# Sinkhorn's column sum behind the second product of a block, its row scaling ahead of the last one, and the first expert's row weights earlier

## The chip, the cores and the metric

The kernel runs on one core of a Trainium2 chip. The metric is the device time of one execution in microseconds (us), and less is better. TensorE is called PE in the rows, VectorE DVE, ScalarE ACT, GpSimd POOL; PEld is TensorE's weight load.

## The reference, cut to what matters

Three stages follow each other: linear attention, a soft mixture of experts, and a second mixture of experts with a Sinkhorn gate. The change touches the last one alone:

```python
logits = x @ w_gate                       # x [2304, 512], w_gate [512, 8]
P = np.exp(logits - logits.max())
for _ in range(8):
    P /= P.sum(1, keepdims=True) + 1e-09  # rows: over the 8 experts
    P /= P.sum(0, keepdims=True) + 1e-09  # columns: over the 2304 tokens
    P *= N / E
for e in range(E):                        # 8 experts
    h = np.maximum(x @ w1[e], 0.0)
    out += P[:, e:e + 1] * (h @ w2[e])
```

## The kernel before

The second mixture runs as 8 experts times 9 blocks of 256 tokens, expert by expert; a block is two row groups of 128 tokens. The matrix product with w2 is done by a Winograd-like scheme in **seven products** (k = 0 to 6) of twelve matmuls each: 4 chunks, each as high part by high weight, high by low, low by high. `PRODUCTS` names for each k the operand (`a11`, `a12`, `s2`, `s1`, `s3`, `s4`, `a22`), the weight part and the running sum (`x`, `z`, `x`, `y`, `x`, `y`, `x`). After each product `take(i, k)` adds the running sum to a quarter of the output tile `xo`. So `x` is read by a take after products 0, 2, 4 and 6, and the next product on `x` cannot write before that read is done. In expert 0 the takes that are first in their quarter are copies on ScalarE (k = 0, 2, 3 and 6) and the others adds on VectorE (k = 1, 4, 5). In experts 1 to 7 all takes are on VectorE and multiply by the token's weight, `xo += P * sum`.

While block i's products run, block i+1's operands are made. After product 2 come the eight matmuls of `first_layer` (z1, then z0), and the generator `hidden` is advanced by one step after each of products 2 to 6: ScalarE makes `r` and the high parts `hh_a`, `hh_s`, VectorE the sums `s1`, `s2`, `s4`, `s3` and the low parts `hl_a`, GpSimd the low parts `hl_s`. The sums and `r` share three buffers.

The next expert's weights are prepared beside this: `W_PARTS` and `W_SUMS` give the (block, product) after which a weight part is cast on ScalarE and its low part made on GpSimd, or a sum of two weights made on GpSimd.

**Sinkhorn** has no stage of its own. It is the generator `sinkhorn`, of which `SINK` advances so many steps after a product, in expert 0 alone. One of the 8 iterations has five steps: (1) row sums `rs`, plus 1e-9, reciprocal; (2) `P` times `rs`; (3) column sums `cs` within each of the 128 partitions; (4) a product with a matrix of ones, `pcs`, that sums over partitions, plus 1e-9, reciprocal, times N / E; (5) `P` times `cs`. With `SINK = {0: 1, 1: 2, 6: 2}` steps 2 and 3 stand after product 6, step 4 after product 0 of the next block, and steps 5 and 1 after its product 1. `pcs` goes into the PSUM tile of z0. The last column sum is in block 8.

`P` is final only at the end of expert 0. Expert 0's `xo` is therefore summed without weight and multiplied by `P[:, t, 0]` afterwards, in `scale_rows`: row groups 0 and 1 after product 4 of expert 0's block 8, the two row groups of each later block behind the last product of the block ahead of it, in expert 1.

From the end of the attention on, every engine works in program order (`InOrder`), so the order in which this loop is written is the order on each engine, and an instruction that waits holds up all that is behind it on its engine.

Of the kernel before, what the change touches and what calls it, by code (L numbers as in the profile page):

```python
# [9 lines left out]
AF = mybir.ActivationFunctionType  # L10
ALU = mybir.AluOpType
# [5 lines left out]
NTOK, DM = B * S, H * D  # L17
NT = NTOK // 128
E, SPE, FF = 8, 4, 1024
# [34 lines left out]
def tile_kernel(ctx: ExitStack, tc: tile.TileContext, a):  # L54
    nc = tc.nc
    PE, V, A, G, SP = nc.tensor, nc.vector, nc.scalar, nc.gpsimd, nc.sync
# [386 lines left out]
    for i in range(NT + LAG + 1):  # L443
        t = i - LAG
# [60 lines left out]
    PE, V, A, G, SP = (InOrder(tc, x) for x in (PE, V, A, G, SP))  # L505
# [93 lines left out]
    NBLK = NT // 2  # L599
# [18 lines left out]
    def w_begin(e):  # L618
        u = [w2_unit("moe2_w2", e, n) for n in range(2)]
        t = cl1.tile([128, KH, 256], F32, tag="t", name=f"t{e}")  # L620
        b11, b12, b21 = u[0][:, :, 0:256], u[0][:, :, 256:512], u[1][:, :, 0:256]
        wsrc[e] = {"b11": b11, "b21": b21, "b22": u[1][:, :, 256:512], "t1": b11, "t2": t, "t3": b12, "t4": b21}
# [31 lines left out]
    def load_munits(n):  # L654
        for _ in range(n):
            if nm[0] < len(munits):
                load_unit(wa, *munits[nm[0]])
                nm[0] += 1
# [64 lines left out]
    xo = cp.tile([128, NT, DM], F32, name="xo")  # L723
    P = cp.tile([128, NT, E], F32, name="P")

    def acc_tile(name):
        return pm.tile([128, 512], F32, tag="m", name=name)

    def z_tile(n, name):
        return pz.tile([128, 1024], F32, tag=f"z{n}", name=name)  # L730
# [17 lines left out]
    def spread_stack(st, e):  # L748

        hl = st[:, FF // 2:].rearrange("p (n f) -> p n f", n=2)  # L750
        for n in range(2):
            pr = z_tile(n, f"pr{e}_{n}")
            for part in range(2):
                for j in range(2):
                    PE.matmul(pr[:, j * 256:(j + 1) * 256], rep[n][:, 2 * j + part, :], hl[:, part, :], start=part == 0 and j == 0, stop=part == 1, skip_group_check=True)
            A.copy(out=st[:, n * 512:(n + 1) * 512], in_=pr[:, 0:512])

    def sinkhorn():

        pg = acc_tile("pgate")  # L760
        for c in range(KC):
            PE.matmul(pg[:, 0:E], sot[:, c, :], wg[:, c, :], start=c == 0, stop=c == KC - 1)
        gst = cp.tile([128, E], F32R, name="gst")
        V.tensor_copy(out=gst, in_=pg[:, 0:E])
        V.tensor_tensor(out=gst[64:128, :], in0=pg[64:128, 0:E], in1=gst[64:128, :].bitcast(F32), op=ALU.subtract)
        yield
        pl = acc_tile("plog")
        for t in range(NT):
            PE.matmul(pl[:, t * E:(t + 1) * E], ct[t // 4][:, t % 4 * 128:(t % 4 + 1) * 128], gst, start=True, stop=True)
        yield  # L770
        Pf = P.rearrange("p t e -> p (t e)")
        V.tensor_copy(out=Pf, in_=pl[:, 0:NT * E])
        gm = cp.tile([128, 1], F32, name="gm")
        V.tensor_reduce(out=gm, in_=Pf, axis=AX.X, op=ALU.max)
        yield
        pg = acc_tile("pgm")
        PE.transpose(pg[0:1, 0:128], gm, ident)
        gm1 = cp.tile([1, 1], F32, name="gm1")
        V.tensor_reduce(out=gm1, in_=pg[0:1, 0:128], axis=AX.X, op=ALU.max)
        pg = acc_tile("pgb")  # L780
        PE.matmul(pg[:, 0:1], ones[0:1, :], gm1, start=True, stop=True)
        yield
        V.tensor_copy(out=gm, in_=pg[:, 0:1])
        V.tensor_scalar_sub(Pf, Pf, gm)
        A.activation(out=P, in_=P, func=AF.Exp)
        yield
        for it in range(8):
            rs = cp.tile([128, NT, 1], F32, tag="rs", name=f"rs{it}")
            V.tensor_reduce(out=rs, in_=P, axis=AX.X, op=ALU.add)
            V.tensor_scalar_add(rs, rs, 1e-9)  # L790
            V.reciprocal(out=rs, in_=rs)
            yield
            V.tensor_tensor(out=P, in0=P, in1=rs.to_broadcast([128, NT, E]), op=ALU.mult)
            yield
            cs = cp.tile([128, 1, E], F32, tag="cs", name=f"cs{it}")
            csf = cs.rearrange("p o e -> p (o e)")
            V.tensor_reduce(out=csf, in_=P.rearrange("p t e -> p e t"), axis=AX.X, op=ALU.add)
            yield
            pg = z_tile(0, f"pcs{it}")
            PE.matmul(pg[:, 0:E], ones, csf, start=True, stop=True)  # L800
            V.tensor_scalar_add(csf, pg[:, 0:E], 1e-9)
            V.reciprocal(out=csf, in_=csf)
            V.tensor_scalar_mul(csf, csf, float(NTOK) / E)
            yield
            V.tensor_tensor(out=P, in0=P, in1=cs.to_broadcast([128, NT, E]), op=ALU.mult)
            yield
# [74 lines left out]
    def product(i, k):  # L881
        e, blk = blocks[i]
        a, _, to = PRODUCTS[k]
        if (i, to) not in sums:
            sums[i, to] = acc_tile(f"{to}_{i}")[:, 0:256]
            fresh = True
        else:
            fresh = False
        h, l = hop.pop((i, a))
        w = wop[e, k]  # L890
        ps = sums[i, to]
        for c in range(KH):
            PE.matmul(ps, h[:, c], w[:, 0, c], start=fresh and c == 0, stop=False, skip_group_check=True)
            PE.matmul(ps, h[:, c], w[:, 1, c], start=False, stop=False, skip_group_check=True)
            PE.matmul(ps, l[:, c], w[:, 0, c], start=False, stop=c == KH - 1, skip_group_check=True)
        if blk == NBLK - 1:
            wop.pop((e, k))

    def take(i, k):

        e, blk = blocks[i]
        ps = sums[i, PRODUCTS[k][2]]
        r, c = TAKES[k]
        t = 2 * blk + r
        o = xo[:, t, c * 256:(c + 1) * 256]
        if e == 0:
            if (r, c) in [TAKES[j] for j in range(k)]:
                V.tensor_tensor(out=o, in0=ps, in1=o, op=ALU.add)
            else:
                (V.tensor_copy if blk == NBLK - 1 else A.copy)(out=o, in_=ps)  # L910
        else:
            V.scalar_tensor_tensor(out=o, in0=ps, scalar=P[:, t, e:e + 1], in1=o, op0=ALU.mult, op1=ALU.add)
        if e == E - 1 and k == 5:
            SP.dma_start(out=a["out"][t * 128:(t + 1) * 128, :], in_=xo[:, t, :])
        if e == E - 1 and (r, c) in ((1, 0), (1, 1)) and k in (4, 6):
            SP.dma_start(out=a["out"][t * 128:(t + 1) * 128, c * 256:(c + 1) * 256], in_=o)

    def scale_rows(blk):
        for t in (2 * blk, 2 * blk + 1):
            A.activation(out=xo[:, t, :], in_=xo[:, t, :], func=AF.Copy, scale=P[:, t, 0:1])  # L920

    sums = {}
    blocks = [(e, blk) for e in range(E) for blk in range(NBLK)]
# [14 lines left out]

    W_SUMS = {(3, 1): 0, (3, 6): 1, (5, 6): 2, (7, 6): 3}
    W_PARTS = {(2, 6): 0, (4, 6): 2, (6, 6): 1, (8, 1): 3, (8, 6): 4, (9, 0): 5, (9, 1): 6}  # L940
    SINK = {0: 1, 1: 2, 6: 2}
    making = iter(())
    for i, (e, blk) in enumerate(blocks):
        more = e + 1 < E
        if blk == 2 and more:
            w_begin(e + 1)
        for k in range(7):
            product(i, k)
            take(i, k)
            if k == 0 and blk == NBLK - 1 and more:  # L950
                stacks[e + 1] = make_stack(e + 1)
            if k == 1 and blk == NBLK - 1 and more:
                spread_stack(stacks[e + 1], e + 1)
            if k == 2 and i + 1 < len(blocks):
                first_layer(i + 1, 1)
                first_layer(i + 1, 0)
                making = hidden(i + 1)
            next(making, None)
            if more and (blk, k) in W_SUMS:
                w_sum(e + 1, W_SUMS[blk, k])  # L960
            if more and (blk, k) in W_PARTS:
                w_part(e + 1, W_PARTS[blk, k])
            if e and (blk + 9, k) in W_PARTS:
                w_part(e, W_PARTS[blk + 9, k])
            if e == 0:
                for _ in range(SINK.get(k, 0) - (blk == 0 and k == 1)):
                    next(sink, None)
            if k == 4 and i + 1 == NBLK:
                scale_rows(0)
        if i + 1 < len(blocks) and blocks[i + 1][0] == 1 and i + 1 > NBLK:  # L970
            scale_rows(blocks[i + 1][1])
        for to in "xyz":
            sums.pop((i, to))
        if blk == 0 and e and more:
            load_munits(4)
# [62 lines left out]
```

## Time and profile before

| | us |
|---|---|
| median of 3 runs | 1099.89 |
| lowest and highest | 1097.52, 1102.34 |
| the profiled execution, its own time | 1099.17 |
| its span, first to last instruction | 1097.0 |
| TensorE busy in the span | 1053.4 |
| expert 0 of the second mixture, its 9 blocks | about 281 to 398 |
| expert 1 | about 398 to 501 |

A matmul's busy time overlaps that of the next one, so TensorE's busy share says little; what counts is the time from the start of a product to the start of the next, and the waits before single instructions. A timeline row gives the start in us from the span's start, the duration, the engine, the line, the operation, output and inputs with shapes, and in brackets the idle time before it with what ended it. Line 50 is a helper that records every operation, so the rows are told apart by their tiles.

### The profile page before, as it was taken

The numbers are of one execution on the slowest core, as the hardware profiler recorded it, in microseconds if no ns is written. First come the engines' busy times: TensorE is split into PE (matmuls) and PEld (weight loads), VectorE is DVE, ScalarE is ACT, GpSimd is POOL, SyncE is SP. The second block draws the span as 40 slices with busy tenths as digits, with TensorE's granted clock in tenths as the row PEclk, the third lists the DMA queues.
The fourth block names the chain that finished last, engine by engine and source line by source line (L and its number), as shares of the span: only waits on it lengthen the run. The fifth ranks groups of instructions, "written<-read, shape, count | busy, mean of one in ns | idle before, by whom it ended". The sixth has DMA issues, their size and how long they took to land.

```text
span 1097.0 us, 23161 instructions
## 1 busy us (share of the span) xinstructions
PE 1053.4 (96%) x9206; PEld 982.4 (90%) x9206; DVE 737.7 (67%) x1526; ACT 569.1 (52%) x1009; POOL 686.8 (63%) x442
## 2 busy tenths in 40 slices
PE   7999999999888899999999999999999999999998
PEld 4788889853888889999999999999999999999998
DVE  6878677750678866766776677567666766676765
ACT  5665544313455556655455455545554564555542
POOL 4776551107555676767767686867677775777443
PEclk9999989999999999999999999999999999999999
DMA  7762215379400040012002200400220022000111
GB/s 261 261 257 85 59 30 208 139 303 370 154 1 1 2 143 12 2 50 105 1 1 78 78 2 1 149 6 2 77 78 1 1 82 73 1 1 21 45 53 59
DMA packets 22571, 89.26 MB, mean 81 GB/s; under 512 B 2752, under 2 KB 5568, under 8 KB 14272
## 3 DMA queue, kind: packets, MB, share of 16 engines
q1 hardware_dynamic: 22176, 87.26, 22.0%
q8 instruction: 73, 1.20, 0.5%
q0 software_dynamic: 288, 0.52, 0.2%
q14 instruction: 34, 0.28, 0.1%
HBM read 83.05 MB, written 4.72 MB: 80 GB/s over the span
## 4 chain that ended last, share of the span: by engine, by line
PE 68%; POOL 15%; issue 6%; DVE 6%; ACT 4%; DMA 1%; SPq 0%; POOLq 0%; ACTq 0%; DVEq 0%
PE x L50 25%; PE y L50 12%; PE z L50 11%; POOL hl_s L50 8%; PE num L271 6%; POOL w_t L50 4%; PE kvacc L179 3%; POOL w_b L50 2%; DVE s L50 2%; PE ut L246 1%; PE ps L50 1%; PE kvp L218 1%; DMA moe_w<-in_moe_w 1%; ACT hh_s L50 1%; DVE xo L50 1%
## 5 line engine op out<-in xcount | busy, mean ns | idle before, releaser
L50 POOL TENSOR_TENSOR hl_s<-s,hh_s 128x512 fp32r<-128x512 f32 x288 | 367.4, 1297 | 240.9 <-ACT hh_s L50 226.5
L50 PE MATMUL x<-w_t,hh_s 128*128 128x256 f32 x1152 | 205.0, 278 | 5.2 <-DVE xo L50 3.9
L50 ACT ACTIVATE hh_s<-s 128x512 fp32r<-128x512 f32 x288 | 175.3, 629 | 52.0 <-DVE s L50 49.3
L50 PEld LDWEIGHTS x<-w_t,hh_s 128*128 128x128 f32 x1152 | 173.9, 188 | 7.2 <-issue 3.2
L50 DVE SCALAR_TENSOR_TENSOR xo<-x,P,xo 128x256 f32<-128x256 f32 x252 | 121.0, 480 | 81.0 <-PE x L50 75.4
L50 ACT ACTIVATE hh_a<-z 128x512 fp32r<-128x512 f32 x216 | 122.2, 600 | 90.5 <-DVE s L50 88.6
L50 ACT ACTIVATE r<-z 128x512 f32<-128x512 f32 x144 | 86.2, 599 | 159.9 <-PE z L50 159.6
L50 DVE SCALAR_TENSOR_TENSOR s<-z,r 128x512 f32<-128x512 f32 x144 | 99.0, 688 | 90.6 <-ACT hh_a L50 86.2
L50 PE MATMUL x<-w_t,hl_s 128*128 128x256 f32 x576 | 159.7, 277 | 0.0
L50 DVE SCALAR_TENSOR_TENSOR hl_a<-z,hh_a 128x512 fp32r<-128x512 f32 x216 | 147.2, 681 | 0.0
L50 DVE SCALAR_TENSOR_TENSOR s<-z,s 128x512 f32<-128x512 f32 x144 | 98.4, 684 | 20.6 <-POOL hl_s L50 19.3
L50 PE MATMUL x<-w_t,hh_a 128*128 128x256 f32 x576 | 104.3, 279 | 5.2 <-POOL w_t L50 4.8
L50 PEld LDWEIGHTS x<-w_t,hl_s 128*128 128x128 f32 x576 | 108.2, 188 | 0.0
L50 PE MATMUL y<-w_b,hh_s 128*128 128x256 f32 x576 | 103.9, 279 | 0.0
L50 PE MATMUL z<-w_b,hh_a 128*128 128x256 f32 x576 | 103.6, 280 | 0.0
L50 PE MATMUL x<-w_b,hh_a 128*128 128x256 f32 x576 | 103.4, 280 | 0.0
L50 PE MATMUL y<-w_t,hh_s 128*128 128x256 f32 x576 | 102.9, 278 | 0.0
L50 PEld LDWEIGHTS x<-w_t,hh_a 128*128 128x128 f32 x576 | 87.6, 188 | 6.8 <-POOL w_t L50 6.2
L50 PEld LDWEIGHTS z<-w_b,hh_a 128*128 128x128 f32 x576 | 87.3, 189 | 2.5 <-issue 2.5
L50 PEld LDWEIGHTS y<-w_b,hh_s 128*128 128x128 f32 x576 | 87.5, 188 | 1.3 <-POOL w_b L50 1.3
L50 PEld LDWEIGHTS x<-w_b,hh_a 128*128 128x128 f32 x576 | 88.0, 190 | 0.0
L50 PEld LDWEIGHTS y<-w_t,hh_s 128*128 128x128 f32 x576 | 87.6, 189 | 0.0
(214 smaller groups left out, 2344.7 us busy)
## 6 DMA issues: line engine op xcount, KB each, us to landing
moe_w<-in_moe_w SPq DMA_DIRECT2D x64, 1024.0 KB, 6.9
vt<-in_vb SPq DMA_DIRECT2D x20, 256.0 KB, 3.6
kt<-in_kT SPq DMA_DIRECT2D x18, 256.0 KB, 3.5
qt<-in_qT SPq DMA_DIRECT2D x18, 256.0 KB, 2.7
out<-xo SPq DMA_DIRECT2D x18, 128.0 KB, 1.7
out<-xo SPq DMA_DIRECT2D x9, 256.0 KB, 2.0
rep<-in_rep POOLq DMA_DIRECT2D x2, 256.0 KB, 6.0
bd<-in_bd SPq DMA_DIRECT2D x1, 384.0 KB, 3.7
```

The costliest lines, as they stand in the source:

```text
L50: return lambda *args, **kwargs: self.tc.keep_in_program_order(make(*args, **kwargs))
L179: PE.matmul(acc[64 * j:64 * j + 64, p * 256:(p + 1) * 256], v[:, (2 * p + j) * D:(2 * p + j + 1) * D], phik[:, 2 * p + j].rearrange("p c f ...
L218: PE.matmul(ps[:, c * 192:(c + 1) * 192], kvt[:, p * 256 + c * 128:p * 256 + (c + 1) * 128], bd[:, p], start=True, stop=True)
L246: PE.transpose(ps[:, j * 128:(j + 1) * 128], uq_t[t][hh][:, j * 128:(j + 1) * 128], ident)
L271: PE.matmul(ps[r0:r1, j * XW:(j + 1) * XW], phiq[:, c, j * 128 + r0:j * 128 + r1], kvs_t[b][:, c, 4 * hh + j, :], start=c == 0, stop=c == 1,)
```

## The change

`SINK` becomes `{1: 3, 5: 2}`. Steps 2 and 3 stand after product 5 now, steps 4, 5 and 1 after product 1 of the next block (in block 0 the first two steps that stood after products 0 and 1 both stand after product 1). In step 4 the addition of 1e-9 and a multiplication by E / N are one instruction ahead of the reciprocal, and the multiplication behind it is gone: eight VectorE instructions fewer in all. `scale_rows` becomes `scale_row`: row group 0 is weighted after product 3 and row group 1 after product 4 of expert 0's block 8; the two row groups of block b+1 are weighted after products 0 and 1 of block b of expert 1, where they were weighted after its product 6.

```diff
             pg = z_tile(0, f"pcs{it}")
             PE.matmul(pg[:, 0:E], ones, csf, start=True, stop=True)
-            V.tensor_scalar_add(csf, pg[:, 0:E], 1e-9)
+            V.tensor_scalar(out=csf, in0=pg[:, 0:E], scalar1=1e-9, scalar2=float(E) / NTOK, op0=ALU.add, op1=ALU.mult)
             V.reciprocal(out=csf, in_=csf)
-            V.tensor_scalar_mul(csf, csf, float(NTOK) / E)
             yield
...
-    def scale_rows(blk):
-        for t in (2 * blk, 2 * blk + 1):
-            A.activation(out=xo[:, t, :], in_=xo[:, t, :], func=AF.Copy, scale=P[:, t, 0:1])
+    def scale_row(t):
+        A.activation(out=xo[:, t, :], in_=xo[:, t, :], func=AF.Copy, scale=P[:, t, 0:1])
...
-    SINK = {0: 1, 1: 2, 6: 2}
+    SINK = {1: 3, 5: 2}
...
-            if k == 4 and i + 1 == NBLK:
-                scale_rows(0)
-        if i + 1 < len(blocks) and blocks[i + 1][0] == 1 and i + 1 > NBLK:
-            scale_rows(blocks[i + 1][1])
+            if i == NBLK - 1 and k in (3, 4):
+                scale_row(k - 3)
+            if e == 1 and k in (0, 1) and blk + 1 < NBLK:
+                scale_row(2 * (blk + 1) + k)
```

In the orders that follow the number behind a name is a serial number of the tile. On **VectorE** in expert 0, around the end of block 1, where block 2's operands are made, the order before is this (`xo<-y` is take 5, `s_2_3593` is s3, `hl_a_2_3589` the low part of a22, `xo<-z` take 1 of block 2):

```order
L50 TENSOR_TENSOR xo<-y_3528,xo 128x256
L50 SCALAR_TENSOR_TENSOR s_2_3593<-z_0_2_3516,r_2_3565 128x512
L50 SCALAR_TENSOR_TENSOR hl_a_2_3589<-z_0_2_3511,hh_a_2_3587 128x512
L50 TENSOR_TENSOR P<-P,rs_3494 128x144
L50 TENSOR_REDUCE cs_3615<-P 128x8
L50 TENSOR_SCALAR cs_3615<-pcs_3632 128x8
L50 RECIPROCAL cs_3615<-cs_3615 128x8
L50 TENSOR_SCALAR cs_3615<-cs_3615 128x8
L50 TENSOR_TENSOR xo<-z_3637,xo 128x256
L50 TENSOR_TENSOR P<-P,cs_3615 128x144
```

and now:

```order
L50 TENSOR_TENSOR xo<-y_3527,xo 128x256
L50 SCALAR_TENSOR_TENSOR s_2_3592<-z_0_2_3515,r_2_3564 128x512
L50 TENSOR_TENSOR P<-P,rs_3493 128x144
L50 TENSOR_REDUCE cs_3596<-P 128x8
L50 SCALAR_TENSOR_TENSOR hl_a_2_3588<-z_0_2_3510,hh_a_2_3586 128x512
L50 TENSOR_TENSOR xo<-z_3631,xo 128x256
L50 TENSOR_SCALAR cs_3596<-pcs_3645 128x8
L50 RECIPROCAL cs_3596<-cs_3596 128x8
L50 TENSOR_TENSOR P<-P,cs_3596 128x144
```

Row scaling and column sums moved ahead of the low part of a22, the reading of `pcs` behind take 1, and the multiplication behind the reciprocal is gone.

On **TensorE** at the start of block 1 of expert 0 (`x<-w_b` is product 0, `z<-w_b` product 1, `x<-w_t,hh_s` product 2) the order before is

```order
L50 MATMUL x_3460<-w_b_2944,hh_a_1_3366 128x256 x2
L50 MATMUL x_3460<-w_b_2944,hl_a_1_3368 128x256
L50 MATMUL pcs_3474<-cs_3458,ones 128x8
L50 MATMUL z_3479<-w_b_3076,hh_a_1_3387 128x256 x2
L50 MATMUL z_3479<-w_b_3076,hl_a_1_3389 128x256
```

and now:

```order
L50 MATMUL z_3474<-w_b_3076,hh_a_1_3387 128x256 x2
L50 MATMUL z_3474<-w_b_3076,hl_a_1_3389 128x256
L50 MATMUL pcs_3488<-cs_3440,ones 128x8
L50 MATMUL x_3460<-w_t_3039,hh_s_1_3409 128x256 x2
L50 MATMUL x_3460<-w_t_3039,hl_s_1_3411 128x256
```

`pcs` moved from between products 0 and 1 to between products 1 and 2. On **ScalarE** from block 8 of expert 0 to block 0 of expert 1 (the names with 9 belong to the operands of expert 1's block 0, `CAST` are weight parts, `xo<-xo,P` is the weighting of a row group, `r_10` begins the operands of block 1) the order before is

```order
L50 ACTIVATE hh_s_9_4691<-s_9_4670 128x512
L50 ACTIVATE hh_s_9_4710<-s_9_4686 128x512
L50 ACTIVATE r_9_4709<-z_1_0_4660 128x512
L50 ACTIVATE xo<-xo,P 128x512 x2
L50 ACTIVATE hh_a_9_4733<-z_1_0_4655 128x512
L50 ACTIVATE hh_s_9_4736<-s_9_4716 128x512
L50 ACTIVATE hh_s_9_4755<-s_9_4739 128x512
L50 CAST w_t_4760<-moe_w_1_0_3298 128x1024
L50 CAST w_b_4777<-moe_w_1_1_3300 128x1024
L50 CAST w_t_4794<-moe_w_1_1_3300 128x1024
L50 ACTIVATE r_10_4820<-z_1_1_4810 128x512
```

and now:

```order
L50 ACTIVATE xo<-xo,P 128x512
L50 ACTIVATE hh_s_9_4703<-s_9_4678 128x512
L50 ACTIVATE r_9_4702<-z_1_0_4652 128x512
L50 ACTIVATE xo<-xo,P 128x512
L50 ACTIVATE hh_a_9_4725<-z_1_0_4647 128x512
L50 ACTIVATE hh_s_9_4728<-s_9_4709 128x512
L50 ACTIVATE hh_s_9_4747<-s_9_4731 128x512
L50 CAST w_t_4752<-moe_w_1_0_3298 128x1024
L50 CAST w_b_4769<-moe_w_1_1_3300 128x1024
L50 ACTIVATE xo<-xo,P 128x512
L50 CAST w_t_4787<-moe_w_1_1_3300 128x1024
L50 ACTIVATE xo<-xo,P 128x512
```

The first two weightings moved apart, and two more, of block 1's row groups, stand in block 0 of expert 1 already. In the later blocks of expert 1 two weightings stand where two stood, but for the row groups of the block that follows. On GpSimd and SyncE the order is the same.

## Rows read from the trace of the kernel before

**Rows 1.** Blocks: stretch, length, busy PE, PEld, DVE, ACT, POOL; clock, DMA.
```profile
307.11:319.48 12.37, 10.97 (x97) 10.80 (x96) 8.54 (x19) 6.09 (x14) 5.12 (x5) 1.00 0.00 1
319.48:332.60 13.12, 11.35 (x96) 10.98 (x95) 12.07 (x19) 7.27 (x15) 10.00 (x7) 1.00 0.00 1
...
420.97:431.45 10.48, 10.48 (x95) 10.48 (x93) 7.30 (x15) 6.27 (x13) 5.10 (x4) 1.00 0.00 0
431.45:442.57 11.12, 10.74 (x94) 10.55 (x93) 7.28 (x15) 7.20 (x13) 9.86 (x6) 1.00 0.01 1
```

**Rows 2.** TensorE's waits, 390 to 480 us: total us, times, longest us.
```profile
PE x L50 <- DVE xo L50: 1.8, 4, 0.7
```

**Rows 3.** Timeline of TensorE, from product 0 to the first layer of block 2, expert 0.
```profile
308.36 0.28 PE L50 MATMUL x<-w_b,hl_a 128*128 128x256 f32 x1
310.04 0.36 PE L50 MATMUL pcs<-cs,ones 128*128 128x8 f32 x2 [1.40 <-DVE cs L50]
310.25 0.49 PE L50 MATMUL z<-w_b,hh_a 128*128 128x256 f32 x2
...
313.07 1.11 PE L50 MATMUL z<-ct,st 128*128 128x256 f32 x8
```

**Rows 4.** Timeline of VectorE over the same stretch.
```profile
307.27 0.69 DVE L50 SCALAR_TENSOR_TENSOR s<-z,r 128x512 f32<-128x512 f32 x1 [0.23 <-POOL hl_s L50]
307.88 0.68 DVE L50 SCALAR_TENSOR_TENSOR hl_a<-z,hh_a 128x512 fp32r<-128x512 f32 x1
308.48 0.96 DVE L50 TENSOR_TENSOR P<-P,rs 128x144 f32<-128x144 f32 x1
309.48 0.41 DVE L50 TENSOR_REDUCE cs<-P 128x8 f32<-128x144 f32 x1
...
312.38 0.31 DVE L50 TENSOR_TENSOR P<-P,cs 128x144 f32<-128x144 f32 x1
...
315.00 0.69 DVE L50 SCALAR_TENSOR_TENSOR s<-z,r 128x512 f32<-128x512 f32 x1 [1.46 <-ACT hh_a L50]
```

**Rows 5.** Timeline of GpSimd, blocks 1 to 3 of expert 0.
```profile
308.00 2.57 POOL L50 TENSOR_TENSOR hl_s<-s,hh_s 128x512 fp32r<-128x512 f32 x2 [0.76 <-DVE s L50]
...
322.91 2.39 POOL L50 TENSOR_TENSOR w_b<-moe_w,w_b 128x1024 fp32r<-128x1024 f32 x1
325.38 2.40 POOL L50 TENSOR_TENSOR moe_w<-moe_w 128x1024 f32<-128x1024 f32 x1
```

**Rows 6.** Timeline of VectorE, block 3 of expert 0.
```profile
323.25 2.08 DVE L50 TENSOR_SCALAR cs<-cs 128x8 f32<-128x8 f32 x1
...
325.58 2.36 DVE L50 TENSOR_TENSOR P<-P,cs 128x144 f32<-128x144 f32 x1
...
328.70 0.63 DVE L50 SCALAR_TENSOR_TENSOR s<-z,r 128x512 f32<-128x512 f32 x1
...
330.64 0.42 DVE L50 TENSOR_TENSOR xo<-x,xo 128x256 f32<-128x256 f32 x1
```

**Rows 7.** Timeline of TensorE, product 6 of block 3, expert 0.
```profile
331.11 0.50 PE L50 MATMUL x<-w_t,hh_a 128*128 128x256 f32 x2 [0.36 <-DVE xo L50]
```

**Rows 8.** Timeline of ScalarE, take 0 of block 3, expert 0.
```profile
321.91 0.38 ACT L50 COPY xo<-x 128x256 f32<-128x256 f32 x1
```

**Rows 9.** Timeline of TensorE, block 8 of expert 0.
```profile
385.02 1.03 PE L50 MATMUL ps<-moe_w,sot 128*32 128x256 f32 x14
387.16 0.36 PE L50 MATMUL pcs<-cs,ones 128*128 128x8 f32 x2 [1.10 <-DVE st L50]
...
388.87 1.10 PE L50 MATMUL pr<-st,rep 128*128 128x256 f32 x8
389.81 0.40 PE L50 MATMUL x<-w_t,hh_s 128*128 128x256 f32 x2
```

**Rows 10.** Timeline of ScalarE, block 8 of expert 0.
```profile
389.54 1.08 ACT L50 CAST st<-pr 128x512 fp32r<-128x512 f32 x2 [5.46 <-PE pr L50]
```

**Rows 11.** Timeline of VectorE, block 3 of expert 1.
```profile
434.17 0.48 DVE L50 SCALAR_TENSOR_TENSOR xo<-x,P,xo 128x256 f32<-128x256 f32 x1 [1.34 <-ACT xo L50]
```

## The prediction, made before the changed kernel ran

> **What bounds the kernel now.** I read the stretches first, block by block, then who waited for whom on TensorE, then the timelines of four engines around the waits. A block of expert 1 in which TensorE waits for nothing is 10.48 us long and is full of its 92 matmuls, 0.114 us from start to start; a block of expert 0 with its column sum is 12.37 us long, though its products are the same [rows 1]. The timeline shows the difference: `pcs`, two tiny matmuls between products 0 and 1, starts 1.68 us behind the start of the last matmul of product 0, at 310.04, where 0.11 would do [rows 3]. It waits for `cs`. The reduction to `cs` ends at 309.89 (309.48 + 0.41), and ahead of it on VectorE stand the low part of a22 and the row scaling, which takes 0.96 us [rows 4], while the same shape, `P` times `cs`, takes 0.31 with GpSimd idle [rows 4]. It ended at 309.44, just behind the first of GpSimd's two `hl_s`, each 1.28 us, the first from 308.00 to 309.28 [rows 5]. So expert 0 is bound by a chain that ends in a two-matmul product, eight times. In expert 1 TensorE waited four times for a take on VectorE, 1.8 us in all [rows 2]; the take itself had waited for the weighting of `xo` on ScalarE, 1.34 us idle [rows 11]. That stretch of 11.12 us is 0.64 longer than the undisturbed one [rows 1].
>
> **The column sum, blocks 1, 2 and 4 to 7.** Of the 1.89 us by which 12.37 exceeds 10.48, 1.57 are the wait (1.68 less one pitch of 0.11), and 0.32 are `pcs` itself with the restart behind it; its two matmuls alone take 0.21 from start to start [rows 3]. `pcs` without a wait was never seen, so its price lies between 0.21 and 0.32; I take 0.32, which leaves a block of 10.80. Now `pcs` is wanted 24 matmuls behind the start of product 0 rather than 12, which without the wait is at about 309.84 (308.36 + 0.11 + 12 pitches). The row scaling moves into the slot of the low part, 307.88 instead of 308.48, right behind s3 [rows 4]. If it gets through there, `cs` is ready at about 308.7 and nothing waits. If it must sit out the first `hl_s`, `cs` is ready at 309.89 as now and `pcs` starts at 310.04: 0.2 us late, 0.3 with a restart. No row has the row scaling ahead of a GpSimd operation, so the cost is 0 to 0.3 a block; the new start is 0.12 ahead of 308.00 [rows 4, 5], and I take 0.
>
> The Trainium skill (SBUF — State Buffer, section "SBUF: two separate sides") says that VectorE instructions with two SBUF inputs and GpSimd share a port pair as an exclusive lock, and that whichever starts first holds it for the whole instruction. By that rule the row scaling wins at 307.88 and the sum stands; by the wait that the row at 308.48 shows, it would be 7 times 0.3, or 2.1 us, worse. The row at 308.48 agrees with the rule for the second comer; no row here shows VectorE first.
>
> The low part of a22 comes some 0.7 to 2.0 us later; its reader, product 6 of the next block, is more than 8 us off, so it costs nothing.
>
> So six blocks gain 1.57 each: **9.4 us**, if nothing else becomes late there. Two things could.
>
> *The chain behind `pcs`.* Take 1, the reading of `pcs`, the reciprocal, `P` times `cs`, and the row sums now stand between product 1 and the next s1, without the wait that gave them room. GpSimd's weight operation runs then, 2.39 us from 322.91 to 325.30, in blocks 3 to 7 [rows 5]. Today the multiplication by N / E sits it out, 2.08 us [rows 6]; that instruction is removed, but `P` times `cs` is then next to sit it out, so its removal brings no more than its own length. A blocked `P` times `cs` ends 0.16 behind GpSimd's end (327.94 against 327.78), and s1 starts 0.76 later [rows 5, 6]. With one such operation s1 therefore starts at 325.30 + 0.92 = 326.22 on the clock of block 3. Undisturbed it starts 1.93 behind the first layer (315.00 against 313.07) [rows 3, 4], and the first layer would stand at 319.48 + 36 pitches + 0.32 = 323.90, so s1 at 325.83. It is 0.39 late. What feels it is product 6, which may not write `x` before take 4 has read it: take 4 ended 2.36 behind the start of s1 (331.06 against 328.70), and product 6 started at 331.11 [rows 6, 7]. That gives take 4 at 328.58, and product 6 is wanted at 323.90 + 44 pitches = 328.91. Covered, with 0.3 to spare; without that cover it would cost what it is late, up to about 0.3 a block.
>
> *Take 0 on ScalarE.* Product 2 needs it. Behind a weight cast it ends at 322.29 [rows 8]; product 2 is wanted at 319.48 + 24 pitches + 0.32 = 322.53. Covered by 0.2; in the three blocks with such a cast up to 0.3 each could be lost.
>
> **Block 3** has two weight operations back to back, until 327.78 [rows 5]. `P` times `cs` gets in between, but the addition of 1e-9 to the row sums, an SBUF operation like the blocked multiplication, then sits out the second. s1 starts at about 328.1, take 4 ends at 330.46 and product 6 starts at 330.5, 1.6 late (2.2 if all is as late as today, 331.11). The block takes 10.80 + 1.6 + 0.1 = 12.5 instead of 13.12 [rows 1]: **0.6 us** (0 to 2.3).
>
> **Block 8.** `pcs` waits there for VectorE to read the stack `ps`, which lies in the same PSUM tile. Product 1 now fills that time from 386.05 on; it takes 1.50 (387.37 to 388.87), so `pr` starts at 387.55 [rows 9]. But `pr` also goes into z0's tile, and `pcs` now stands behind it: it must wait for the first of the two casts of `pr`, which ends 1.2 us behind its start (389.54 + 0.54 against 388.87) [rows 9, 10]. `pcs` starts at 388.8 and product 2 at 389.1 instead of 389.81: **0.7 us** (0.4 to 1.0).
>
> **Expert 1's weightings.** They keep their place on ScalarE but serve the block that follows, so take 0 no longer waits. Blocks 3, 5 and 7 gain 0.64 each, 1.92; in block 1, which holds the longest wait [rows 2], VectorE is late for other reasons too, and I take 0.4 of 0.7: **2.3 us** (1.9 to 2.6). Two weightings come into block 0, where ScalarE's first layer work may start 0.5 later; GpSimd's weight parts are what that block waits for, so I cost it at nothing.
>
> **Sum.** 9.4 + 0.6 + 0.7 + 2.3 = 13.0 us. The profiled execution, 1099.17 (span 1097.0 and 2.2 around it), becomes 1086.2. It lies 0.7 under the median of 1099.89, so from the median **1086.9**.
>
> **The rivals.**
>
> 1. *The margins don't hold.* The row scaling sits out `hl_s` as today (7 times 0.3), and product 6 or product 2 waits 0.3 in five blocks. Gain 13.0 - 2.1 - 1.5 - 0.6 in block 3 = 8.8: about 1091. For it: margins of 0.2 to 0.3. Against: the new order starts the scaling first.
> 2. *Every block becomes like block 3.* If the row sums' addition misses its turn in blocks 4 to 7 too, each loses 1.7: gain 13.0 - 6.8 - 1.5 = 4.7, 1095. Against: GpSimd has one operation there, then nothing for 3 us or more.
> 3. *The wait moves instead of going.* If the operands, not `pcs`, set expert 0's period, only expert 1 gains: 1097.5. Against: expert 1 makes the same operands in 10.48 us [rows 1].
> 4. *Slower.* The row scaling has no claim on the port: if it misses both turns between GpSimd's operations and also sits out the weight operation, `pcs` starts at 325.30 + 0.16 + 0.41 + 0.15 = 326.0 instead of 322.2, 3.8 us in each of blocks 3 to 7, 19 us against the 13.0: 1106. It decides from four such blocks on. Against: it got in at the first turn [rows 4, 5].
>
> That the edit does something else than it says is excluded by the order of the instructions.
>
> **Chances.** Forecast 0.60, rival 1 0.27, rival 2 0.05, rival 3 0.04, rival 4 0.04. 0.5% is 5.5 us, about what a measurement can tell from no change: faster 0.87, same 0.09, slower 0.04. The range holds the forecast and rival 1. Low end: `pcs` at 0.21 in seven blocks (0.8), block 1 and block 8 at their best (0.6), block 3 without its stall (1.7): 1084. High end: rival 1 and a run's scatter of 1: 1092.
>
> **What would show it.** In the trace after: no wait of over 0.3 us ahead of `pcs` in blocks 1 to 7; `P` times `rs` at about 0.31 us; `P` times `cs` at up to 2.4 in blocks 3 to 7; product 6 of block 3 late behind take 4; blocks 1 and 2 of 10.8 us; no wait ahead of product 2 in blocks 3, 5 and 7 of expert 1. The prediction is wrong if blocks of expert 0 stay above 11.5 us.

## The result and the profile after

The changed kernel takes 1085.99 us (median of 4 runs, 1084.86 to 1089.08) against 1099.54 us before (4 runs, 1097.52 to 1102.34): a ratio of 0.987, 95% interval 0.985 to 0.9891, faster by 13.6 us. In the profiled executions it is 1086.30 against 1099.17, 12.9 less, and the span fell from 1097.0 to 1084.1. The prediction's 1086.9, worked out from a median of 1099.89 before, is 0.9 above the median measured.

The stretches, product 0 to product 0, of single blocks after; the columns are those of [rows 1]: length, busy time of PE, PEld, DVE, ACT and POOL, granted clock, DMA.

```profile
306.43:317.19 10.76, 10.76 (x96) 10.76 (x95) 7.67 (x18) 6.08 (x14) 5.16 (x5) 1.00 0.00 1
317.19:329.64 12.45, 11.03 (x96) 10.83 (x95) 11.12 (x18) 7.24 (x15) 10.01 (x7) 1.00 0.00 1
329.64:340.40 10.76, 10.76 (x96) 10.76 (x95) 9.39 (x19) 6.31 (x14) 7.33 (x6) 1.00 0.01 2
...
420.44:430.92 10.48, 10.48 (x95) 10.48 (x93) 7.18 (x14) 7.03 (x13) 9.72 (x6) 1.00 0.01 2
```

Block 2 of expert 0 fell from 12.37 to 10.76 us and is now full of TensorE's work; block 3 fell from 13.12 to 12.45 only; block 3 of expert 1 (the last row) fell from 11.12 to 10.48.

The whole stage, in the kernel before: blocks 1 to 7 of expert 0, its block 8, block 0 of expert 1, blocks 1 to 7 of expert 1.

```profile
294.73:382.62 87.89, 77.60 (x661) 76.23 (x659) 70.44 (x133) 45.73 (x95) 50.21 (x35) 1.00 0.01 1
382.62:397.58 14.96, 13.86 (x136) 12.76 (x135) 10.01 (x22) 8.44 (x16) 9.89 (x6) 1.00 0.38 141
397.58:409.41 11.83, 11.13 (x95) 10.73 (x93) 6.13 (x13) 7.42 (x12) 11.09 (x7) 1.00 0.34 100
409.41:486.08 76.67, 74.86 (x647) 74.06 (x645) 52.49 (x101) 47.51 (x82) 50.93 (x35) 1.00 0.04 13
```

The same four after:

```profile
295.67:372.93 77.26, 75.84 (x660) 75.64 (x659) 64.05 (x126) 46.40 (x95) 50.25 (x35) 1.00 0.01 1
372.93:387.17 14.24, 14.03 (x136) 12.77 (x135) 9.13 (x21) 8.55 (x17) 9.88 (x6) 1.00 0.40 148
387.17:398.78 11.61, 10.90 (x94) 10.64 (x93) 6.09 (x13) 8.36 (x13) 11.05 (x7) 1.00 0.33 102
398.78:473.05 74.27, 73.83 (x647) 73.66 (x645) 52.54 (x101) 47.64 (x82) 50.97 (x35) 1.00 0.04 14
```

That is 10.63 + 0.72 + 0.22 + 2.40 = 13.97 us gained. Block 1 starts 0.94 us later (295.67 against 294.73): 0.78 of that lies ahead of expert 0 (its products start at 281.98 against 281.20), where the code is the same, and 0.16 in block 0 (13.69 against 13.53; 13.49 when the changed kernel was run again, so this is scatter). Behind block 7 of expert 1 the program takes 0.13 us more than before. 13.97 less 0.94 is 13.0, and the spans differ by 12.9.

VectorE around the end of block 1 and the first part of block 2 after, as [rows 4]:

```profile
306.62 0.69 DVE L50 SCALAR_TENSOR_TENSOR s<-z,r 128x512 f32<-128x512 f32 x1 [0.25 <-POOL hl_s L50]
307.23 0.30 DVE L50 TENSOR_TENSOR P<-P,rs 128x144 f32<-128x144 f32 x1
307.56 0.43 DVE L50 TENSOR_REDUCE cs<-P 128x8 f32<-128x144 f32 x1
307.90 0.69 DVE L50 SCALAR_TENSOR_TENSOR hl_a<-z,hh_a 128x512 fp32r<-128x512 f32 x1
```

and GpSimd's pair beside it, as [rows 5]:

```profile
307.33 2.59 POOL L50 TENSOR_TENSOR hl_s<-s,hh_s 128x512 fp32r<-128x512 f32 x2 [0.75 <-DVE s L50]
```

The row scaling starts 0.10 ahead of GpSimd's first `hl_s` and takes 0.30 us, where it took 0.96 when it started 0.48 behind. `cs` is ready at 307.99. TensorE over product 1's end, as [rows 3], takes `pcs` at 309.16 without a wait, 0.12 behind the start of the matmul ahead:

```profile
309.04 0.28 PE L50 MATMUL z<-w_b,hl_a 128*128 128x256 f32 x1
309.16 0.28 PE L50 MATMUL pcs<-cs,ones 128*128 128x8 f32 x2
309.30 0.48 PE L50 MATMUL x<-w_t,hh_s 128*128 128x256 f32 x2
```

In block 3, as [rows 6], VectorE is held up twice: `P` times `cs` takes 2.25 us where it took 0.31 in block 2, and the addition of 1e-9 to the row sums 1.97 where it took 0.18.

```profile
320.95 2.25 DVE L50 TENSOR_TENSOR P<-P,cs 128x144 f32<-128x144 f32 x1
323.24 0.30 DVE L50 TENSOR_REDUCE rs<-P 128x18 f32<-128x144 f32 x1
323.58 1.97 DVE L50 TENSOR_SCALAR rs<-rs 128x18 f32<-128x18 f32 x1
...
325.77 0.63 DVE L50 SCALAR_TENSOR_TENSOR s<-z,r 128x512 f32<-128x512 f32 x1
```

and product 6 pays for it, as [rows 7]:

```profile
328.18 0.50 PE L50 MATMUL x<-w_t,hh_a 128*128 128x256 f32 x2 [1.42 <-DVE xo L50]
```

### The profile page after: what moved, and what is told of

Read it like the earlier page. It is cut to its first block, busy times and chain, and to the rows that moved or that the text cites. A ratio compares the mean times of both kernels' runs of the same rounds, so it can differ in the third digit from the quotient of the medians.

```text
span 1084.1 us, 23152 instructions
## 1 busy us (share of the span) xinstructions
PE 1052.2 (97%) x9206; PEld 982.0 (91%) x9206; DVE 732.0 (68%) x1518; ACT 569.8 (53%) x1009; POOL 687.3 (63%) x442
## 4 chain that ended last, share of the span: by engine, by line
PE 78%; POOL 11%; DVE 5%; issue 2%; DMA 2%; ACT 1%; SPq 0%; POOLq 0%; DVEq 0%; ACTq 0%
PE x L50 30%; PE y L50 14%; PE z L50 12%; PE num L271 6%; POOL hl_s L50 5%; POOL w_t L50 3%; PE kvacc L179 3%; POOL w_b L50 2%; PE ut L246 1%; PE ps L50 1%; DVE s L50 1%; PE kvp L218 1%; DMA moe_w<-in_moe_w 1%; PE pk L142 1%; PE ph L50 1%
```

## The experiments

The theory: the gain is the wait ahead of `pcs`, which goes because `cs` is ready earlier (the row scaling gets ahead of GpSimd's `hl_s`) and is wanted later; what is left in block 3 comes from the addition to the row sums, held up by GpSimd's second weight operation; expert 1 gains because take 0 no longer waits for a weighting. The rivals: the eight multiplications that are gone carried the gain; the place of `pcs` alone carries it; the place of the row scaling does nothing; block 3 simply has too much work.

One sentence on the measure: the stretch from 240 us to the start of expert 0's products, in which nothing was changed, was 40.0 to 46.0 us long in the profiled executions, so effects of 1 to 2 us are read from the stretches of blocks, and the times of whole runs stand beside them. The kernel before was run again beside each set of experiments, which gave 1099.78 for the first four and 1100.64 for the others.

### The steps alone

Against the kernel before:

```diff
-    SINK = {0: 1, 1: 2, 6: 2}
+    SINK = {1: 3, 5: 2}
```

> Only the Sinkhorn steps moved; the multiplication behind the reciprocal stays, the weightings stay where they were before. Theory (the gain is the wait ahead of pcs, about 1.6 us in each of blocks 1 to 7 of expert 0, and 0.7 in block 8): blocks 1 and 2 of 10.76 us as in the changed kernel, block 3 about 0.65 longer than there (13.1), because the multiplication takes the turn between GpSimd's two weight operations and P times cs then sits out the second; blocks of expert 1 as before. Gain over before 10.7 us, time about 1088.8. Rival (the gain comes from the eight VectorE multiplications that are gone, five of which took 2.08 us): then only the weightings' and the moved steps' small change shows, under 3 us, time 1096.5 or more.

Measured: 1087.76 us against 1099.78 (ratio 0.9899, 0.9884 to 0.9915). Blocks 1 to 7 and, apart, block 3:

```profile
293.97:371.76 77.79, 76.24 (x660) 75.97 (x659) 64.81 (x133) 46.55 (x95) 50.26 (x35) 1.00 0.01 1
...
315.49:328.09 12.60, 11.05 (x96) 10.85 (x95) 11.24 (x19) 7.26 (x15) 10.14 (x7) 1.00 0.01 1
```

10.1 us are gained in blocks 1 to 7, and block 8 takes 14.24 as in the changed kernel, so the steps carry all of expert 0's gain but 0.5 us. The rival of the multiplications falls. Of the expectation block 3 was a miss: 12.6, not 13.1. VectorE's rows there show why:

```profile
319.25 2.10 DVE L50 TENSOR_SCALAR cs<-cs 128x8 f32<-128x8 f32 x1
321.38 0.31 DVE L50 TENSOR_TENSOR P<-P,cs 128x144 f32<-128x144 f32 x1
...
322.06 1.92 DVE L50 TENSOR_SCALAR rs<-rs 128x18 f32<-128x18 f32 x1
```

The multiplication sat out the first weight operation, and `P` times `cs` still slipped in behind it, at 321.38, so only one more wait, that of the addition, was left. GpSimd's row for the second operation is this:

```profile
321.40 2.55 POOL L50 TENSOR_TENSOR moe_w<-moe_w 128x1024 f32<-128x1024 f32 x1
```

It started 0.02 behind `P` times `cs` and took 2.55 us instead of 2.40 [rows 5]. In all five blocks with a weight operation the multiplication took about 2.1 us here and `P` times `cs` 0.31; in the changed kernel, without the multiplication, `P` times `cs` takes 2.23 to 2.26 in them, and VectorE's busy time is only 0.8 us less (64.05 against 64.81).

### The fused instruction alone

Against the kernel before:

```diff
-            V.tensor_scalar_add(csf, pg[:, 0:E], 1e-9)
+            V.tensor_scalar(out=csf, in0=pg[:, 0:E], scalar1=1e-9, scalar2=float(E) / NTOK, op0=ALU.add, op1=ALU.mult)
             V.reciprocal(out=csf, in_=csf)
-            V.tensor_scalar_mul(csf, csf, float(NTOK) / E)
```

> Only the fused instruction: the multiplication is gone, steps and weightings stand as before. Theory: pcs still waits 1.4 us in blocks 1 to 7; P times cs sits out GpSimd's weight operation in place of the multiplication, except in block 3, where s1 comes about 0.6 earlier, so 0.5 us gained there. Gain 0 to 0.7 us, time about 1099. Rival (the multiplications carried the gain): 5 times 2.08 us or a good part of it, time 1089 to 1095.

Measured: 1098.89 us against 1099.78, ratio 0.9991 (0.9978 to 1.0004), no difference by the times. VectorE is busy 61.92 us in blocks 1 to 7, 8.5 less than before, and the blocks are 0.67 shorter:

```profile
293.46:380.68 87.22, 77.30 (x661) 76.13 (x659) 61.92 (x127) 45.62 (x95) 50.22 (x35) 1.00 0.01 1
...
318.30:330.77 12.47, 11.05 (x97) 10.89 (x95) 10.26 (x18) 7.16 (x15) 9.89 (x7) 1.00 0.01 1
```

0.65 of it lies in block 3, the second row: 12.47 instead of 13.12. The expectation was right in the time and wrong in the way to it: `P` times `cs` did not take over the whole wait. In blocks 3 to 7 it takes 0.73 to 0.78 us, not 2.1. Block 3:

```profile
323.22 0.42 DVE L50 TENSOR_TENSOR xo<-z,xo 128x256 f32<-128x256 f32 x1 [1.18 <-PE z L50]
323.56 0.74 DVE L50 TENSOR_TENSOR P<-P,cs 128x144 f32<-128x144 f32 x1
```

Take 1 stands ahead of it in this order and cannot start before product 1 is done, so VectorE sits idle for 1.18 us instead of being held up, and `P` times `cs` meets only the end of GpSimd's weight operation. Eight and a half microseconds of VectorE's time were worth 0.7 us. In blocks 3 to 7 VectorE is idle 1.13 to 1.18 us ahead of take 1 instead, and TensorE, which waits for `pcs` in every block as before, waited for a take in block 3 alone, 0.36 us ahead of its product 6 [rows 7]; that wait is gone.

### The weightings alone

The edit of the changed kernel to `scale_rows`, with Sinkhorn as before:

```diff
...
-            if k == 4 and i + 1 == NBLK:
-                scale_rows(0)
-        if i + 1 < len(blocks) and blocks[i + 1][0] == 1 and i + 1 > NBLK:
-            scale_rows(blocks[i + 1][1])
+            if i == NBLK - 1 and k in (3, 4):
+                scale_row(k - 3)
+            if e == 1 and k in (0, 1) and blk + 1 < NBLK:
+                scale_row(2 * (blk + 1) + k)
```

> Only the weightings of xo moved; Sinkhorn as before. Theory: the four waits of product 2 in blocks 1, 3, 5 and 7 of expert 1 go (block 3: 11.12 to 10.48 us), 2.4 us there and 0.2 in block 0; expert 0 as before (12.37 us a block). Gain 2.6, time about 1096.9. Rival (the weightings cost ScalarE the same time wherever they stand, and the gain in expert 1 comes from expert 0 ending earlier): no change, 1099.5.

Measured: 1097.92 us against 1099.78, ratio 0.9984 (0.9967 to 1.0001), which the times alone leave open. The stretches don't: blocks 1 to 7 of expert 0, block 0 and then blocks 1 to 7 of expert 1:

```profile
295.44:383.44 88.00, 77.66 (x661) 76.28 (x659) 70.51 (x133) 45.80 (x95) 50.18 (x35) 1.00 0.00 1
...
398.40:410.01 11.61, 10.90 (x95) 10.64 (x93) 6.09 (x13) 8.36 (x13) 11.05 (x7) 1.00 0.34 102
410.01:484.31 74.30, 73.85 (x647) 73.68 (x646) 52.55 (x101) 47.66 (x82) 51.01 (x35) 1.00 0.04 14
```

Expert 0 is as before (88.0 against 87.9), expert 1 as in the changed kernel: 0.22 in block 0 and 2.37 behind it. The parts of the change, 10.1 + 0.7 for the steps, 2.6 for the weightings, and 0.5 for the fused instruction on top of the steps, add up to 13.9 of the 13.97. The rival that expert 1 gains only because expert 0 ends earlier is refuted.

### pcs later, row scaling where it was

Against the changed kernel:

```diff
-    SINK = {1: 3, 5: 2}
+    SINK = {1: 3, 6: 2}
```

> The changed kernel, but row scaling and column sums stay behind product 6, that is behind the low part of a22; pcs stands behind product 1. Theory (the row scaling is in time only when it starts ahead of GpSimd's first hl_s; behind its start it sits it out): P times rs takes 0.95 us again, cs is ready 0.05 us after product 1 ends, pcs waits about 0.2 with 0.1 restart in blocks 1 to 7. Blocks of about 11.0 us, 2 us less gain than the changed kernel, time about 1088. Rival (the place of pcs alone carries the gain): blocks of 10.76 us, time 1086.

Measured: 1089.95 us against 1099.78 (0.9912, 0.9892 to 0.9933). Blocks 1 to 7:

```profile
298.65:377.89 79.24, 77.44 (x660) 76.07 (x659) 69.37 (x126) 45.72 (x95) 50.45 (x35) 1.00 0.01 1
```

2.0 us more than the changed kernel's 77.26, six blocks at 11.0 to 11.3. On VectorE the row scaling is back behind the low part and takes 0.97 us; GpSimd's pair started at 310.59, 0.49 ahead of it:

```profile
310.59 2.61 POOL L50 TENSOR_TENSOR hl_s<-s,hh_s 128x512 fp32r<-128x512 f32 x2 [0.75 <-DVE s L50]
```

```profile
310.48 0.68 DVE L50 SCALAR_TENSOR_TENSOR hl_a<-z,hh_a 128x512 fp32r<-128x512 f32 x1
311.08 0.97 DVE L50 TENSOR_TENSOR P<-P,rs 128x144 f32<-128x144 f32 x1
312.08 0.43 DVE L50 TENSOR_REDUCE cs<-P 128x8 f32<-128x144 f32 x1
```

`pcs` starts at 312.67, 0.38 behind the start of the matmul ahead where 0.12 would do. At 0.30 us the scaling would have had `cs` ready 0.67 earlier, in time for `pcs`. So the place of `pcs` is not all: 0.28 to 0.36 us in each of the six blocks hang on which of the two engines starts first (block 3, late for its own reason, takes 12.47).

### Row scaling sooner, pcs where it was

Against the changed kernel:

```diff
-    SINK = {1: 3, 5: 2}
+    SINK = {0: 1, 1: 2, 5: 2}
```

> The changed kernel, but pcs, its reciprocal and the two steps behind it stay where they were before (pcs between products 0 and 1); row scaling and column sums stand behind product 5. Theory: cs is ready some 0.35 us behind the end of product 0 rather than 1.57, so pcs waits 0.35 with 0.1 restart: blocks of about 11.2 us, and block 8 waits for the reading of ps again (0.7). Gain 13.5 less 3.1 less 0.7, time about 1090. Rival (row scaling finds GpSimd in its way wherever it stands, and only the later place of pcs helps): blocks of 12.3 us, time 1097.

Measured: 1092.24 us against 1100.64 (0.9919, 0.9896 to 0.9942). A block, the reduction to `cs` in it, and the wait at its `pcs`:

```profile
310.68:321.93 11.25, 11.06 (x97) 10.89 (x95) 7.63 (x18) 6.09 (x14) 5.13 (x5) 1.00 0.00 1
```

```profile
311.81 0.45 DVE L50 TENSOR_REDUCE cs<-P 128x8 f32<-128x144 f32 x1
```

```profile
311.93 0.28 PE L50 MATMUL x<-w_b,hl_a 128*128 128x256 f32 x1
312.40 0.36 PE L50 MATMUL pcs<-cs,ones 128*128 128x8 f32 x2 [0.19 <-ACT hh_s L50]
```

`pcs` is 0.47 behind the matmul ahead, 0.36 late as worked out. The row names ScalarE's `hh_s`, which `pcs` doesn't read; the reduction to `cs` ends at 312.26, and `pcs` follows 0.14 later, as it did 0.15 later in the kernel before (309.89 to 310.04). Block 8 is back to 14.91. Blocks 1 to 7 take 79.86 us. Either half of the move, with the rest of the change, brings at least 8.0 us of the 10.6 in blocks 1 to 7, and both together take the last 2.0 to 2.6. The profiled execution lost time ahead of the stage (last section), so its whole-run time says less than its blocks.

### The row sums without their 1e-9

The addition to the row sums is left out; nothing else differs from the changed kernel.

```diff
             V.tensor_reduce(out=rs, in_=P, axis=AX.X, op=ALU.add)
-            V.tensor_scalar_add(rs, rs, 1e-9)
             V.reciprocal(out=rs, in_=rs)
```

> The changed kernel without the addition of 1e-9 to the row sums, which is left out of the computation. Theory (in block 3 that addition sits out GpSimd's second weight operation, s1 comes 1.7 us late and product 6 waits 1.6 for take 4): the reciprocal isn't held up, s1 stands at most 0.4 late, block 3 falls from 12.45 to about 10.8 us, the other blocks stay at 10.76. Time 1.65 us under the changed kernel, about 1084.3. Rival (block 3 is late because VectorE or GpSimd has too much to do in it): block 3 loses no more than the 0.2 us of the instruction.

Measured: 1082.92 us against 1100.64 (0.9844, 0.9822 to 0.9865). Block 3 falls from 12.45 to 10.78, with GpSimd as busy in it (9.94 us) as in the changed kernel:

```profile
315.04:325.82 10.78, 10.78 (x97) 10.78 (x96) 9.27 (x17) 7.00 (x15) 9.94 (x7) 1.00 0.01 2
```

Its VectorE waits once, 2.26 us for `P` times `cs`, and s1 starts at 321.62, 0.52 behind the row sums' start at 321.10 rather than 2.53 (323.24 to 325.77 in the changed kernel). One instruction of 0.18 us that reads and writes SBUF cost the block 1.67 us; that block 3 has too much work is refuted.

### The weight operations apart

Against the changed kernel, for the weights of expert 1 alone: the first weight part is made one block earlier, in block 2, and the first sum stays in block 3, so that GpSimd has one weight operation in each. Nothing is left out:

```diff
+    LATE = W_SUMS, W_PARTS
+    EARLY = {**W_SUMS, (2, 6): 0}, {**W_PARTS, (1, 6): 0}
+    EARLY[0].pop((3, 1))
+    EARLY[1].pop((2, 6))
...
-        if blk == 2 and more:
+        W_SUMS, W_PARTS = LATE if e else EARLY
+        if blk == (2 if e else 1) and more:
             w_begin(e + 1)
```

> The changed kernel; in expert 0 alone the first weight part is made one block earlier (behind product 6 of block 1) and the first weight sum behind product 6 of block 2, so that no block has two weight operations on GpSimd back to back at its start. Nothing is left out. Theory: block 3 falls from 12.45 to 10.76 us, block 2 stays at 10.76 to 10.9 (it has a weight cast ahead of take 0 now). Time 1.6 us under the changed kernel, about 1084.4. Rival (too much work in the block, not the order): block 2 gains what block 3 loses, no change.

Measured: 1084.92 us against 1100.64 (0.9867, 0.9845 to 0.9889). The changed kernel, run again beside it:

> The changed kernel again, as the measure for the run with the spread weight operations on the same chip: 1086.0, 13.5 us under before.

Measured: 1087.13 us (0.9874, 0.9852 to 0.9896). The intervals overlap, so the times don't tell the two apart; the blocks do. Blocks 1 to 7, then blocks 2 and 3 alone, of the kernel with the operations apart:

```profile
294.58:370.12 75.54, 75.54 (x661) 75.54 (x659) 64.09 (x126) 46.57 (x95) 50.37 (x35) 1.00 0.01 2
...
305.34:316.10 10.76, 10.76 (x97) 10.76 (x96) 9.40 (x18) 7.19 (x15) 7.52 (x6) 1.00 0.00 1
316.10:326.86 10.76, 10.76 (x97) 10.76 (x96) 9.39 (x18) 6.28 (x14) 7.52 (x6) 1.00 0.01 2
```

1.7 us less than the changed kernel's 77.26: block 3 is down to 10.76 and block 2 gave nothing for it. TensorE waits for nothing in these seven blocks. By its blocks it is the best version here that leaves nothing out.

## Why the prediction held, step by step

- **The wait ahead of pcs, 6 times 1.57.** Right, and a little small. Blocks 1, 2, 4, 5 and 6 take 10.76 us against 10.80 forecast, block 7 11.01. The six gained 9.96 against 9.4: the price of `pcs` without a wait, bounded at 0.21 to 0.32 and taken at 0.32, is 0.28 (10.76 less 10.48), so each gained 0.04 more, and the other 0.3 is that blocks 4, 6 and 7 took 12.46 to 12.68 before, not 12.37.
- **The row scaling gets through first.** Taken at no cost, 0 to 0.3 a block. Right: 0.30 us at 307.23, and 0.30 in all eight iterations. The run with the scaling behind the low part shows the other end: 2.0 us over seven blocks, where the prediction had 2.1.
- **The Trainium skill's rule** (SBUF — State Buffer, "SBUF: two separate sides"), that of VectorE and GpSimd the one that starts first keeps the shared ports for the whole instruction, agrees now on VectorE's side: the scaling that starts 0.10 ahead takes 0.30. On GpSimd's side it agrees in part only. The weight operation that starts 0.02 behind `P` times `cs` takes 0.15 longer (2.55 instead of 2.40), though 0.29 us of `P` times `cs` were still to come; the two `hl_s` that start 0.10 behind the scaling take 2.59 together, as against 2.57 before, though 0.20 of the scaling were to come. That GpSimd waits for the whole instruction isn't shown here.
- **The removed multiplication brings next to nothing by itself.** Right: 0.53 us on top of the moved steps, where the wait passed to `P` times `cs` (2.23 to 2.26 us in blocks 3 to 7), as worked out, and 0.67 us by itself, nearly all in block 3. There the wait passed on only in part, because take 1 stood in between; the time of VectorE that this freed lay idle.
- **Product 6 covered in blocks 4 to 7.** Right: no wait there, nor at product 2 behind the casts. Block 7's 11.01 is no such wait: TensorE waits for nothing in it, and block 7 of expert 1, which has no column sum, is 0.21 above its neighbours too (10.69).
- **Block 3, 0.6 us.** Right in size and cause: 13.12 to 12.45, with product 6 1.42 us idle behind take 4. The run without the addition and the one with the weight operations apart both take the whole stall away.
- **Block 8, 0.7 us.** Right: 14.96 to 14.24. `pcs` waits 0.21 us for the first cast of `pr`:

```profile
377.77 1.09 PE L50 MATMUL pr<-st,rep 128*128 128x256 f32 x8
379.08 0.39 PE L50 MATMUL pcs<-cs,ones 128*128 128x8 f32 x2 [0.21 <-ACT st L50]
```

- **Expert 1, 2.3 us.** A little small: 2.62. Behind block 0 it is 2.40 against 2.32 worked out. Block 0, costed at nothing, gained 0.22. The run with the weightings alone gained the same 0.22, so it belongs to them. In that block GpSimd's three weight parts run back to back and TensorE waits for the last, before and after; that the chain ahead of them is shorter through the split of the two weightings in block 8 was not tried by itself.
- **The rivals.** Rival 1's margins held (no wait in blocks 4 to 7); rival 2 is what block 3 alone does; rival 3 is refuted by blocks full of TensorE's work; for rival 4 no row shows a scaling that missed a turn.

The sum of the steps, 13.0, stands against 13.97 in the stretches: the six blocks and expert 1 were costed 0.5 and 0.3 too low. That the profiled executions differ by 12.9, almost the 13.0 forecast, is luck: one of them lost 0.94 us ahead of block 1, which the change does not explain. The medians' 13.55 holds the same scatter.

## What to carry to other kernels

A tiny product between large ones costs them the whole wait for its operand, about 1.6 us a block here, and 0.28 us if its operand is ready. Count both ends: how much later it can be wanted and how much earlier its operand can be ready. Look also at which engine starts first where VectorE and GpSimd both work from SBUF: `P` times `cs` took 0.31 us when it started 0.02 ahead of a weight operation, and 2.25 when it started 0.31 behind one. An instruction that spends 2 us held up is not 2 us to be had. Take it away, and either the next of its kind takes over the wait, as in the changed kernel, or the engine waits for something else instead, as with the fused instruction alone. Moving the work that holds it up did bring the time back: 1.7 us in block 3.

## What the runs showed of the hardware that was not expected

GpSimd can lose time to VectorE too, if little: 0.15 us in the row at 321.40, where VectorE as the second comer lost up to 2 us. That rests on one row.

The stretch ahead of expert 0's products, in which expert weights arrive, scattered by 6 us between profiled executions of kernels that have the same code there. From 240 us to that start: with the row sums' addition left out, with the row scaling as before, and with `pcs` as before:

```profile
240.00:280.02 40.02, 35.86 (x391) 17.72 (x383) 5.99 (x25) 14.04 (x24) 27.12 (x16) 0.99 0.91 363
```

```profile
240.00:285.06 45.06, 40.66 (x380) 21.55 (x372) 5.89 (x25) 13.88 (x23) 27.05 (x16) 0.84 0.88 348
```

```profile
240.00:285.98 45.98, 41.32 (x418) 20.47 (x410) 6.70 (x29) 14.28 (x24) 27.40 (x17) 0.91 0.88 354
```

The granted clock, the column behind POOL, is 0.99 in the short one and 0.84 and 0.91 in the long ones, so part of their time ran at the lower level, 1.2 GHz of the two levels of 1.2 and 2.4, while DMA was busy at 0.88. The clock is not all of it: the longest of the three is not the one with the lowest clock. What brings the clock down in one execution and not in the next, these runs don't say.
